# Attention before two mixture-of-experts layers: which engine computes the bias rows of the first tile, and how four PSUM banks are handed out

## Chip, cores, metric

The program runs on 1 core of one Trainium2 chip. The metric is the device time of one execution in microseconds (us); lower is better.

## What is computed

The reference, cut to the attention, where the change is. Batch B = 2, heads H = 8, sequence S = 576, head size D = 64.

```python
scores = scale * np.matmul(q, k.transpose(0, 1, 3, 2))
psi_rel = np.log1p(np.abs(pos[:, None] - pos[None, :]))
psi_i = np.log1p(np.maximum(pos[:, None], 1.0))
x = (psi_rel / psi_i)[..., None]
h = np.maximum(x @ w1 + b1, 0.0)          # 32 hidden units
bias = h @ w2                             # one number per head
scores = scores + bias.transpose(2, 0, 1)[None]
attn = np.exp(scores - scores.max(-1, keepdims=True))
attn = attn / (attn.sum(-1, keepdims=True) + 1e-09)
attn_out = np.matmul(attn, v)
```

The result goes through a first feed-forward layer and a second one with 8 experts, of which each token uses two. The change touches neither.

## The kernel before

**Tiling of the attention.** The 576 queries are cut into tiles of 128 (t = 0 to 3) and a rest of 64 per batch element. `BLOCKS` is the list of (batch, tile), the tile outermost, so the two batch elements share a tile's bias. A step of the main loop is a "pair" p: one block and two heads. There are 36 pairs.

**The bias.** The bias of a tile comes from 8 groups G of 16 queries. For a group, `bias_relu` writes four rows of 128 x 576 (g = 0 to 3): each is a shifted window of a table `wl`, plus a constant per partition, under a relu. Then `bias_mm` (L1048) multiplies them by `w2b` into PSUM, `bias_copy` scales the result into an SBUF tile `bt`, and `bias_store` (L1069, queue of SP) carries it by DMA into the tile `bias`. Groups 0 to 7 make the bias of tile t = 0, without which no pair can begin its softmax. Groups 8 and 9 follow right behind, and group 10 + p is made during pair p, for tiles 1 to 3.

**Who makes the rows.** For G < `POOLED` = 5, ACT makes row 3 (L1036) and DVE rows 0 to 2 (L1038). They lie in the later probability buffers (`pp`, even groups) or in four buffers `u` (odd groups). For G >= 5 POOL makes all four rows (L1034) in eight buffers `up`, that is, it can be two groups ahead of TensorE (PE). POOL has no add with relu here: it computes min and max with the constant, so the group's constant is negated (L995) and what is missing is added in the copy (`self.c`, L1060 on ACT for tile 0, L1062 on DVE after it). The first tile is computed in the order of groups 0, 5, 1, 2, 6, 3, 4, 7.

**A pair.** `qk` (L1138) writes the scores of two heads into two PSUM tiles `sc` (there are two such tiles of two banks each). `add_bias` (L1149, DVE) adds the bias and finds the extremum, `exp` (L1162, ACT) writes `pp`, `inv` (L1169 to L1172, DVE) makes the reciprocal of the sum, `tp` (L1181, L1183, PE) transposes the probabilities in three tiles of 128 x 384 or 512, `tp_copy` (L1189, ACT) copies each out as `pts`, `pv` (L1206, PE) multiplies them by v, and `pv_out` (L1217, DVE) writes the result. On PE the order of a steady pair is: `qk` of the next pair, three `tp`, two halves of a group's `bias_mm`, `pv`.

**The four PSUM banks.** The transposes, the halves of the bias from group 8 on, and the `pv` output all take a tile named `m` from the pool `ps_m` with four buffers of one bank each. All have one name, so the pool picks one of the four that it holds to be free when a tile is asked for.

**What sets the order.** Each engine runs its instructions in the order in which they are issued. A planner (`Plan`) takes the list of steps with costs, dependencies and keys, and fixes that order before the program runs. For the planner, tiles `m` go strictly in turn (`slot("m", 4)`); which bank a tile really gets is the pool's choice.

Of the kernel before, what the change touches and what calls it, by code (L numbers as in the profile page):

```python
# [9 lines left out]
F32 = mybir.dt.float32  # L10
# [8 lines left out]
P = 128  # L19
# [19 lines left out]

WL1 = TABS[0][0] - 103 - P  # L40

POOLED = 5


def group_of(G):
# [926 lines left out]
class Attn:  # L972
    def __init__(self, ctx, tc, t, xa, xb, ident):
        self.tc, self.nc = tc, tc.nc
        self.t = t
        self.ident = ident
        self.xa, self.xb = xa, xb
        nc = self.nc
        cp = ctx.enter_context(tc.tile_pool(name="aconst", bufs=1))
        self.wk = ctx.enter_context(tc.tile_pool(name="awork", bufs=2))  # L980
        self.early = ExitStack()
        self.wk2 = self.early.enter_context(tc.tile_pool(name="aearly", bufs=2, side="right"))
        self.ps_sc = ctx.enter_context(tc.tile_pool(name="ps_sc", bufs=2, space=bass.MemoryType.PSUM))
        self.ps_m = ctx.enter_context(tc.tile_pool(name="ps_m", bufs=4, space=bass.MemoryType.PSUM))
        self.small = small = cp.tile([P, SMALL], F32, name="small")
        nc.sync.dma_start(small, t["small"])

        self.wl = cp.tile([P, TABS[0][1]], F32, name="wl")
        nc.scalar.dma_start(self.wl[:, WL1:], t["psi0"][:, WL1:])
        self.w2b = small[:, 2:34]  # L990
        self.ninv = small[:, 34:34 + SEQ // 16]
        self.scb = small[:, 34 + SEQ // 16:-1]
        n = 4 * POOLED
        nc.vector.tensor_scalar(self.scb[:, :n], self.scb[:, :n], small[:, 1:2], None, op0=OP.mult)
        nc.vector.tensor_scalar(self.scb[:, n:], self.scb[:, n:], small[:, 1:2], -1.0, op0=OP.mult, op1=OP.mult)  # L995
        self.c = small[:, SMALL - 1:]
        self.scale_wl(slice(WL1, TABS[0][1]))

        self.kp = [cp.tile([P, 2, 4, SEQ], F32R, name=f"kp{b}") for b in range(2)]
        self.vt = [cp.tile([P, 4, 4, 2, 64], F32, name=f"vt{b}") for b in range(2)]  # L1000
        self.v5 = [cp.tile([P, 4, 2, 64], F32, name=f"v5{b}") for b in range(2)]

        self.bias, self.U, self.B, self.Q, self.S, self.PP, self.PT, self.X, self.raw = ({} for _ in range(9))

    def scale_wl(self, s):
        self.nc.vector.tensor_scalar(self.wl[:, s], self.wl[:, s], self.small[:, 0:1], None, op0=OP.mult)
# [2 lines left out]
    def groups(self, t):  # L1009
        return range(8 * t, min(8 * t + 8, SEQ // 16))  # L1010

    def constant(self):

        nc = self.nc
        cb = self.ps_m.tile([P, 512], F32, name="m")
        for g in range(4):
            nc.tensor.matmul(cb[32 * g:32 * g + 32, 0:1], self.w2b, self.small[:, 1:2], start=True, stop=True)
        nc.vector.tensor_scalar(self.c, cb[:, 0:1], -1.0, None, op0=OP.mult)
# [22 lines left out]
    def bias_mm(self, G, halves):  # L1041
        if len(halves) == 2:
            bp = self.ps_sc.tile([P, 2, 512], F32, name="sc")
        else:
            bp = self.ps_m.tile([P, 512], F32, name="m")[:, None, :]
        for k, n in enumerate(halves):
            for g in range(4):
                self.nc.tensor.matmul(bp[32 * g:32 * g + 32, k, :288], self.w2b,  # L1048
                                      self.U[G, g][:, n * 288:(n + 1) * 288], start=True, stop=True)
        self.B[G, halves] = bp  # L1050
# [123 lines left out]
    def tp(self, blk, c, k):  # L1174


        p = self.PP[blk, c][0]
        pt = self.ps_m.tile([P, 512], F32, name="m").rearrange("p (a b) -> p a b", a=4)
        for j in range(3):
            o = (3 * k + j) * P  # L1180
            self.nc.tensor.transpose(pt[:, j, :], p[:, o:o + P], self.ident)  # L1181
        if k == 2:
            self.nc.tensor.transpose(pt[:, 3, :], self.X.pop(("i", blk, c)).rearrange("p a b -> p (a b)"), self.ident)  # L1183
        self.PT[blk, c, k] = pt
# [7 lines left out]
    def pv(self, blk, c):  # L1192

        self.PP.pop((blk, c))
        pts = [self.PT.pop((blk, c, k)) for k in range(3)]
        xt = self.ps_m.tile([P, 512], F32, name="m")[:, :P]
        self.X[blk, c] = xt, pts[2][:, 3, :]
        for b, o, n in self.parts(blk):
            cs = slice(o, o + n)
# [28 lines left out]
    def run(self, late, moe):  # L1228
# [28 lines left out]
        def rows(G, key):  # L1257
            t, i, _ = group_of(G)
            us = []
            for g in range(4):  # L1260
                us.append(slot("up", 8) if G >= POOLED else slot("u", 4) if G % 2 else ("pp", g // 2, g % 2))
                e = "POOL" if G >= POOLED else "ACT" if g == 3 else "DVE"
                add(e, {"ACT": .67, "DVE": .43, "POOL": .75}[e], self.bias_relu, (G, g, e), [("wl", 0)] if t > 1 else [],
                    [us[-1]], key + .1 * g)
            return us

        def group(G, us, key):
# [12 lines left out]
        q(0)  # L1280
        kc(0, 0)

        for i, G in enumerate((0, 5, 1, 2, 6, 3, 4, 7)):
            group(G, rows(G, i - 9.7), i - 9)
            if i == 3:
                kc(0, 1, [("st", 2)])
# [22 lines left out]
        def v(b, c, after=()):  # L1309
            add("SP", 1.1, self.load_v, (b, c), list(after), [("v", b, c)], 4 * b + c - 1, 2.0)  # L1310

        qk(0)
        landed = [("st", 7)]
        v(0, 0, landed)
# [152 lines left out]
```

## Time and profile before

| | us |
|---|---|
| runs shown, median of 3 | 685.68 (684.35 to 686.38) |
| profiled execution, own time | 689.21 |
| its span in the trace | 687.5 |
| PE busy | 654.7 (95%) |
| DVE busy | 458.0 (67%) |
| ACT busy | 342.9 (50%) |
| POOL busy | 180.9 (26%) |

The profiled execution took 3.5 us longer than the median of the runs, and 1.7 us of its own time lie outside the span. The attention fills about the first 199 us; the two feed-forward layers follow. Shares of busy time are means over stages with quite different limits, so the rows below are those of single stretches.

### The profile page before, as it was taken

How to read it: one execution, taken by the hardware profiler on the slowest of the kernel's cores; microseconds unless marked ns; L12 is line 12 of the kernel's file. 1: busy time of each engine (PE TensorE's matmuls, PEld its weight loads, DVE VectorE, ACT ScalarE, POOL GpSimd, SP SyncE). 2: the span in 40 equal slices, each digit the busy share in tenths (PEclk: the TensorE clock that was granted, in tenths of full speed). 3: DMA queues.
4: the chain of work that ended last, by engine and by line, in shares of the span. 5: the costliest groups of instructions: out<-in, count | busy, mean ns of one | idle time of the engine just before them, and what ended most of it. 6: DMA issues, size and time to landing. Idle time of an engine off the chain costs nothing.

```text
span 687.5 us, 14783 instructions
## 1 busy us (share of the span) xinstructions
PE 654.7 (95%) x5777; PEld 553.0 (80%) x5777; DVE 458.0 (67%) x1010; ACT 342.9 (50%) x657; POOL 180.9 (26%) x215
## 2 busy tenths in 40 slices
PE   6799999999999998999999999999999999999992
PEld 2467766777789987999988997898888889888881
DVE  7589887976879878946656435565656465565621
ACT  5367766676674333445545345544434444444420
POOL 6867655541000000000042003103133140403311
PEclk9889999999999999999999999999999999999997
DMA  3785862326356787735245404658585776858521
GB/s 115 200 231 167 272 208 69 91 54 212 110 185 184 224 242 240 247 89 184 77 155 157 128 31 139 214 185 257 173 247 172 239 215 198 273 174 270 167 66 40
DMA packets 41629, 118.60 MB, mean 173 GB/s; under 512 B 6100, under 2 KB 6356, under 8 KB 39506
## 3 DMA queue, kind: packets, MB, share of 16 engines
q1 hardware_dynamic: 36850, 105.47, 49.8%
q0 software_dynamic: 4560, 11.71, 5.1%
q8 instruction: 47, 0.77, 0.5%
q10 hardware_dynamic: 144, 0.41, 0.2%
q14 instruction: 28, 0.23, 0.1%
HBM read 77.91 MB, written 30.75 MB: 158 GB/s over the span
## 4 chain that ended last, share of the span: by engine, by line
PE 79%; DVE 9%; DMA 5%; ACT 3%; issue 2%; POOL 0%; DVEq 0%; ACTq 0%; POOLq 0%
PE h L312 28%; PE acc L584 17%; PE m L1206 5%; PE sc L1138 5%; PE m L1181 4%; PE m L1048 4%; PE acc L344 4%; PE acc L342 3%; PE acc L343 3%; DMA wr<-in_w_in 3%; ACT pts L1189 2%; PE acc L523 1%; DMA wr<-in_w_out 1%; PE acc L380 1%; PE sc L1048 1%
## 5 line engine op out<-in xcount | busy, mean ns | idle before, releaser
L286 DVE TENSOR_TENSOR wlo<-wr,whi 128x1024 fp32r<-128x1024 f32 x96 | 117.1, 1222 | 55.9 <-ACT whi L283 51.4
L312 PE MATMUL h<-xah,whi 128*128 128x320 f32 x384 | 120.5, 314 | 0.3 <-DVE gg L329 0.3
L283 ACT ACTIVATE whi<-wr 128x1024 fp32r<-128x1024 f32 x96 | 101.2, 1056 | 36.4 <-PE acc L584 13.3
L312 PE MATMUL h<-xal,whi 128*128 128x320 f32 x384 | 119.1, 310 | 0.1
L312 PE MATMUL h<-xah,wlo 128*128 128x320 f32 x384 | 118.6, 309 | 0.0
L1034 POOL TENSOR_SCALAR up<-wl,small 128x576 f32<-128x576 f32 x124 | 96.9, 798 | 55.8 <-PE m L1048 46.0
L584 PE MATMUL acc<-whi,g 128*128 128x512 f32 x320 | 106.7, 398 | 0.0
L618 POOL DMA_INDIRECT out<-row x24 | 35.4, 1475 | 178.9 <-DVE row L609 140.2
L312 PEld LDWEIGHTS h<-xah,whi 128*128 128x128 f32 x384 | 72.4, 189 | 7.9 <-DVE gg L329 1.4
L558 ACT ACTIVATE g<-h 128x320 fp32r<-128x320 f32 x64 | 28.0, 437 | 98.8 <-PE h L312 43.9
L473 POOL DMA_INDIRECT xs<-rows,sidx x18 | 20.2, 1120 | 213.0 <-ACT lk L326 145.0
L312 PEld LDWEIGHTS h<-xal,whi 128*128 128x128 f32 x384 | 72.4, 189 | 4.5 <-DVE xal L545 0.9
L584 PE MATMUL acc<-wlo,g 128*128 128x512 f32 (+1 forms) x192 | 75.7, 395 | 0.0
L312 PEld LDWEIGHTS h<-xah,wlo 128*128 128x128 f32 x384 | 72.3, 188 | 0.0
L565 DVE SCALAR_TENSOR_TENSOR g<-h,g 128x64 fp32r<-128x64 f32 (+1 forms) x128 | 35.4, 318 | 51.9 <-ACT g L558 50.9
L1189 ACT ACTIVATE pts<-m 128x384 f32<-128x384 f32 (+1 forms) x108 | 50.0, 523 | 38.7 <-PE m L1181 35.2
L584 PEld LDWEIGHTS acc<-whi,g 128*128 128x128 f32 x320 | 56.9, 188 | 8.7
L344 PE MATMUL acc<-whi,g 128*128 128x512 f32 x144 | 56.8, 394 | 2.4 <-DVE g L333 2.4
L342 PE MATMUL acc<-whi,g 128*128 128x512 f32 x144 | 57.5, 399 | 0.0
L1162 ACT ACTIVATE pp<-s,mn 128x576 f32<-128x576 f32 x72 | 54.9, 767 | 5.1 <-DVE mn L1149 5.1
L343 PE MATMUL acc<-wlo,g 128*128 128x512 f32 x144 | 57.1, 396 | 0.0
L1149 DVE CUSTOM_DVE_ANT_0 s<-sc,bias 128x576 f32<-128x576 f32 x72 | 51.4, 747 | 1.1 <-PE sc L1138 1.1
(160 smaller groups left out, 1212.4 us busy)
## 6 DMA issues: line engine op xcount, KB each, us to landing
wr<-in_w SPq DMA_DIRECT2D x64, 512.0 KB
bias<-bt SPq DMA_DIRECT2D x40, 288.0 KB
wr<-in_w_in SPq DMA_DIRECT2D x8, 1024.0 KB
wr<-in_w_out SPq DMA_DIRECT2D x8, 1024.0 KB
wf<-wr SPq DMA_DIRECT2D x16, 512.0 KB
wr<-wf SPq DMA_DIRECT2D x16, 512.0 KB
row<-xs SPq DMA_DIRECT2D x23, 258.0 KB
xs<-xb SPq DMA_DIRECT2D x4, 1290.0 KB
```

Of the source, the lines that this page charges most:

```text
L283: self.nc.scalar.activation(w[0], r, AF.Copy)
L286: self.nc.vector.tensor_tensor(out=lo, in0=r, in1=hi.bitcast(F32), op=OP.subtract)
L312: self.nc.tensor.matmul(h, u[:, d, :], v[:, d, :], start=(d == 0 and i == 0), stop=(d == DC - 1 and i == 2))
L342: nc.tensor.matmul(acc, gh, whi, start=(f == 0), stop=False)
L343: nc.tensor.matmul(acc, gh, wlo, start=False, stop=False)
L344: nc.tensor.matmul(acc, gl, whi, start=False, stop=(f == self.FF1 // P - 1))
L565: self.nc.vector.scalar_tensor_tensor(gl, h[:, c], 0.0, g[:, c].bitcast(F32), op0=OP.max, op1=OP.subtract)
L584: nc.tensor.matmul(y, u, v, start=(f == 0 and i == 0), stop=(last and i == len(prods) - 1))
L1034: self.nc.gpsimd.tensor_scalar(u, w, 3.0e38, b, op0=OP.min, op1=OP.max)
L1149: self.nc.vector.tensor_tensor_reduce(out=s.rearrange("p (a b) -> p a b", a=2), in0=sc[:, :, :288], in1=bias[:, h, :].rearrange("p (a b) - ...
L1162: self.nc.scalar.activation(p[:, a * SEQ:(a + 1) * SEQ], s, AF.Exp, bias=mn[:, 0:1], scale=-1.0, accum_out=sm[:, 0, a:a + 1])
L1189: self.nc.scalar.activation(ps, self.PT[blk, c, k][:, :n, :], AF.Copy)
```

## The change

1. `POOLED` goes from 5 to 8. All groups of the first tile (0 to 7) now have three rows on DVE and one on ACT; POOL makes rows from group 8 on. The groups of the first tile run in the order 0 to 7.
2. The negation of POOL's constants, and the scaling of the 128 columns of `wl` that only later tiles read, move out of the set-up into a step `negate` on DVE. All POOL rows of tile 1 wait for it. It is planned behind row 2 of group 6; in the order that comes out it stands behind all 24 DVE rows.
3. The pool of four tiles `m` becomes four tiles m0 to m3 of one buffer each, and `bank()` takes them strictly in turn.

```diff
-POOLED = 5
+POOLED = 8
...
-        self.ps_m = ctx.enter_context(tc.tile_pool(name="ps_m", bufs=4, space=bass.MemoryType.PSUM))
+        self.ps_m = ctx.enter_context(tc.tile_pool(name="ps_m", bufs=1, space=bass.MemoryType.PSUM))
+        self.banks = 0
...
-        nc.vector.tensor_scalar(self.scb[:, n:], self.scb[:, n:], small[:, 1:2], -1.0, op0=OP.mult, op1=OP.mult)
         self.c = small[:, SMALL - 1:]
-        self.scale_wl(slice(WL1, TABS[0][1]))
+        self.scale_wl(slice(WL1 + P, TABS[0][1]))
...
+    def bank(self):
+
+        self.banks += 1
+        return self.ps_m.tile([P, 512], F32, name=f"m{self.banks % 4}")
...
+    def negate(self):
+
+        n = 4 * POOLED
+        self.nc.vector.tensor_scalar(self.scb[:, n:], self.scb[:, n:], self.small[:, 1:2], -1.0, op0=OP.mult, op1=OP.mult)
+        self.scale_wl(slice(WL1, WL1 + P))
...
-        cb = self.ps_m.tile([P, 512], F32, name="m")
+        cb = self.bank()
...
-            bp = self.ps_m.tile([P, 512], F32, name="m")[:, None, :]
+            bp = self.bank()[:, None, :]
...
-        pt = self.ps_m.tile([P, 512], F32, name="m").rearrange("p (a b) -> p a b", a=4)
+        pt = self.bank().rearrange("p (a b) -> p a b", a=4)
...
-        xt = self.ps_m.tile([P, 512], F32, name="m")[:, :P]
+        xt = self.bank()[:, :P]
...
-                add(e, {"ACT": .67, "DVE": .43, "POOL": .75}[e], self.bias_relu, (G, g, e), [("wl", 0)] if t > 1 else [],
-                    [us[-1]], key + .1 * g)
+                add(e, {"ACT": .67, "DVE": .43, "POOL": .75}[e], self.bias_relu, (G, g, e), [("neg", 0)] * (t > 0) + [("wl", 0)] * (t > 1),
+                    [us[-1], (f"row{G}.{g}", 0)], key + .1 * g)
...
-        for i, G in enumerate((0, 5, 1, 2, 6, 3, 4, 7)):
+        for i, G in enumerate(range(8)):
...
+        add("DVE", .5, self.negate, (), [("row6.2", 0)], [("neg", 0)], -2.2)
```

**What moves on DVE, at the start.** The order of the program before, from the first row of the bias to the first `add_bias` (`ql` and `kp` are the low halves of the split q and k):

```order
L1038 TENSOR_SCALAR pp<-wl,small 128x576 x3
L1038 TENSOR_SCALAR u<-wl,small 128x576 x3
L1109 SCALAR_TENSOR_TENSOR ql<-raw,qh 128x512
L1038 TENSOR_SCALAR pp<-wl,small 128x576 x3
L1083 TENSOR_TENSOR kp_97<-raw,kp_97 128x576
L1038 TENSOR_SCALAR u<-wl,small 128x576 x3
L1038 TENSOR_SCALAR pp<-wl,small 128x576 x3
L1062 TENSOR_SCALAR bt<-m,small 128x288 x2
L1083 TENSOR_TENSOR kp_97<-raw,kp_97 128x576
L1062 TENSOR_SCALAR bt<-m,small 128x288 x2
L1149 ISA s,mn<-sc,bias 128x576
```

The same stretch of the changed program (lines have shifted by 11; L1020 is the negation, the L1011 behind it the 128 columns of `wl`):

```order
L1049 TENSOR_SCALAR pp<-wl,small 128x576 x3
L1049 TENSOR_SCALAR u<-wl,small 128x576 x3
L1120 SCALAR_TENSOR_TENSOR ql<-raw,qh 128x512
L1094 TENSOR_TENSOR kp_96<-raw,kp_96 128x576
L1049 TENSOR_SCALAR pp<-wl,small 128x576 x3
L1020 TENSOR_SCALAR small<-small 128x112
L1011 TENSOR_SCALAR wl<-wl,small 128x128
L1094 TENSOR_TENSOR kp_96<-raw,kp_96 128x576
L1073 TENSOR_SCALAR bt<-m_303,small 128x288
L1073 TENSOR_SCALAR bt<-m_308,small 128x288
L1160 ISA s,mn<-sc,bias 128x576
```

Rows that repeat stand once: there are now eight triples of rows where there were five. The negation stands behind all of them, and one `bt` pair (group 9) now comes behind the two `add_bias`.

**What moves on PE, in two pairs of the middle.** Before, behind the last `qk` of a block in the second batch element, the three transposes of a pair and the bias halves behind them, with the semaphores that each waits for:

```order
L1181 MATMUL m<-ident,pp 128x128 [waits PE_49,Activation_49]
L1181 MATMUL m<-ident,pp 128x128 x2
L1181 MATMUL m<-ident,pp 128x128 [waits Activation_49]
L1183 MATMUL m<-ident,inv 128x128 [waits DVE_49]
L1048 MATMUL m<-up,small 32x288 [waits Pool_49] x4
L1048 MATMUL m<-up,small 32x288 x4
```

And the same pair now:

```order
L1192 MATMUL m_1768<-ident,pp 128x128 [waits PE_49,Activation_49]
L1192 MATMUL m_1780<-ident,pp 128x128 [waits DVE_49]
L1192 MATMUL m_1780<-ident,pp 128x128 [waits Activation_49]
L1192 MATMUL m_1786<-ident,pp 128x128 [waits DVE_49]
L1194 MATMUL m_1786<-ident,inv 128x128 [waits DVE_49]
L1059 MATMUL m_1796<-up,small 32x288 [waits DVE_49,Pool_49]
L1059 MATMUL m_1804<-up,small 32x288 [waits Activation_49]
```

Before, the second and the third transpose began with a wait for ACT alone; now they begin with a wait for DVE, as they do in the other pairs of both programs, and the wait for ACT inside the second is the one for the second head's `pp`. The pair after this one reads the same before and after.

## Rows read from the trace of the kernel before

**Rows 1.** The page, chain that ended last: shares of the span by engine.

```profile
PE 79%; DVE 9%; DMA 5%; ACT 3%; issue 2%; POOL 0%; DVEq 0%; ACTq 0%; POOLq 0%
```

**Rows 2.** DVE, the bias rows of L1038: duration ns min/median/max, first and last start us.

```profile
L1038 DVE TENSOR_SCALAR pp<-wl,small x9: 520/995/1002, 6.1 to 19.5; 128x576 f32<-128x576 f32 x9
L1038 DVE TENSOR_SCALAR u<-wl,small x6: 916/996/996, 8.3 to 16.8; 128x576 f32<-128x576 f32 x6
```

**Rows 3.** Timeline of DVE, first 21 us: start, us, what, count.

```profile
5.40 0.63 DVE L1006 TENSOR_SCALAR wl<-wl,small 128x807 f32<-128x807 f32 x1
...
11.09 0.68 DVE L1109 SCALAR_TENSOR_TENSOR ql<-raw,qh 128x512 fp32r<-128x512 f32 x1
...
14.36 0.74 DVE L1083 TENSOR_TENSOR kp<-raw,kp 128x576 fp32r<-128x576 f32 x1
...
17.70 2.83 DVE L1038 TENSOR_SCALAR pp<-wl,small 128x576 f32<-128x576 f32 x3
```

**Rows 4.** Timeline of POOL, its bias rows.

```profile
6.14 15.72 POOL L1034 TENSOR_SCALAR up<-wl,small 128x576 f32<-128x576 f32 x16 [4.76 <-DVE wl L1006]
22.44 2.90 POOL L1034 TENSOR_SCALAR up<-wl,small 128x576 f32<-128x576 f32 x4 [0.58 <-PE sc L1048]
...
40.57 3.92 POOL L1034 TENSOR_SCALAR up<-wl,small 128x576 f32<-128x576 f32 x4 [1.33 <-PE m L1048]
```

**Rows 5.** Timeline of ACT: a row, a copy, and the last copy of tile 0.

```profile
16.34 0.77 ACT L1036 ACTIVATE pp<-wl,small 128x576 f32<-128x576 f32 x1
17.01 0.82 ACT L1060 ACTIVATE bt<-sc,small 128x576 f32<-128x576 f32 x1
...
22.84 0.83 ACT L1060 ACTIVATE bt<-sc,small 128x576 f32<-128x576 f32 x1 [0.26 <-PE sc L1048]
```

**Rows 6.** Chain of waits in order of time, from the last store of tile 0.

```profile
23.70 3.65 DMA bias<-bt
...
27.38 0.98 DVE bt L1062 x2
28.36 0.66 DVE s L1149
```

**Rows 7.** Timeline of PE: groups 8 and 9, and the `qk` that open pairs.

```profile
24.71 2.15 PE L1048 MATMUL m<-up,small 128*32 128x288 f32 x32
29.18 1.50 PE L1138 MATMUL sc<-kp,qh 64*128 64x288 f32 x4 [2.32 <-DVE mn L1149]
...
37.01 0.54 PE L1138 MATMUL sc<-kp,qh 64*128 64x288 f32 x4
...
49.55 0.53 PE L1138 MATMUL sc<-kp,qh 64*128 64x288 f32 x4
```

**Rows 8.** Timeline of DVE: end of the `inv` that PE awaits before 49.55.

```profile
45.13 0.23 DVE L1172 COPY inv<-sm 128x128 f32<-128x128 f32 x1
```

**Rows 9.** Busy time by stretch: us, PE, PEld, DVE, ACT, POOL, granted clock, DMA, GB/s.

```profile
29.00:36.50 7.50, 7.22 (x66) 5.22 (x70) 4.21 (x14) 5.11 (x12) 3.65 (x6) 0.55 0.84 262
...
43.00:49.50 6.50, 4.94 (x63) 3.31 (x62) 5.55 (x14) 4.45 (x11) 3.33 (x3) 0.74 0.90 237
```

**Rows 10.** Timeline of PE: four `qk` in a row, and transposes between them.

```profile
94.47 0.54 PE L1138 MATMUL sc<-kp,qh 64*128 64x288 f32 x4
...
98.90 0.53 PE L1138 MATMUL sc<-kp,qh 64*128 64x288 f32 x4
...
101.09 0.55 PE L1181 MATMUL m<-ident,pp 128*128 128x128 f32 x3 [0.64 <-ACT pts L1189]
...
105.06 0.54 PE L1138 MATMUL sc<-kp,qh 64*128 64x288 f32 x4
...
111.21 0.54 PE L1138 MATMUL sc<-kp,qh 64*128 64x288 f32 x4
```

**Rows 11.** Timeline of ACT in the first of those two pairs.

```profile
99.88 0.63 ACT L1106 ACTIVATE qh<-raw 128x512 fp32r<-128x512 f32 x1 [0.90 <-PE sc L1138]
100.54 0.49 ACT L1189 ACTIVATE pts<-m 128x384 f32<-128x384 f32 x1
```

## Prediction

> **What bounds the kernel now.** I read the chain of waits first. PE carries 79% of it [rows 1], and in the middle of the attention PE runs without a gap in a fixed rhythm, but for two pairs (term 3): one `qk` to the next takes 98.90 - 94.47 = 4.43 us [rows 10]. So whatever delays PE early moves everything behind it, and the change can act in two places only: the head of the program, where PE waits for the bias of the first tile, and single pairs where PE waits for a bank. The feed-forward layers hang on the end of the attention (their first weight loads wait for buffers that it frees), so I carry a shift to the end in full.
>
> The head, in order. DVE makes 15 rows. The shortest took 520 ns, the middle one 995 [rows 2]; the short one is the very first, at 6.1, and POOL began its own rows at 6.14 [rows 4]. Three rows at 17.70 took 2.83, a pitch of (2.83 - 0.995)/2 = 0.92 [rows 3]. POOL's 16 rows took 15.72, 0.98 each, while four rows with DVE idle took 2.90, 0.725 each [rows 4]. The two engines slow each other; nothing else in the rows differs. DVE's last row ends at 17.70 + 2.83 = 20.53, ACT's last copy of tile 0 at 22.84 + 0.83 = 23.67 [rows 5], the store lands at 27.35, and DVE first spends 0.98 on a copy of group 9, so `add_bias` starts about 28.3 [rows 6]. PE, done with groups 8 and 9 at 26.86, stands still for 2.32 and starts the next `qk` at 29.18 [rows 7], with a granted clock of 0.55 until 36.5 [rows 9], mostly the lower of its two levels (1.2 GHz, not 2.4). That `qk` to the next takes 37.01 - 29.18 = 7.83 in place of 4.43.
>
> **Term 1, DVE's rows.** Nine rows are added (24 for 15), but POOL is silent beside them. The price of a row alone shows once: 0.52 long. Successive DVE rows overlap by 0.995 - 0.92 = 0.08, which makes the pitch 0.44; the scaling of `wl`, 807 columns in 0.63 just before POOL starts [rows 3], gives 0.45 for 576 columns. I take 0.44, with 0.52 as the upper end. Rows and the two splits between them (0.68 and 0.74 long [rows 3], 1.27 together less the overlap) are 24 x 0.44 + 1.27 = 11.8; begun at 5.97 (the scaling covers 679 columns, 0.1 shorter), DVE ends at 17.8, 2.7 earlier than now. At 0.52 it is 19.7. ACT does eight rows and eight copies at 0.67 a piece (17.01 - 16.34 [rows 5]), 10.7, plus three splits of some 0.6, from 5.9: 18.4 without any wait, and it waits some 1.5 for its first copies. So ACT is nearly as tight as DVE: the last copy ends at about 20.1 against 23.67, the store lands 3.65 later at 23.8, and `add_bias` begins there, since group 9's copy now stands behind it: 4.5 earlier.
>
> The Trainium skill ("SBUF — State Buffer", Who interferes with whom) says that of a DVE instruction that uses the pair of ports shared with GpSimd and a GpSimd instruction the later one blocks until the other is done. By that a DVE row beside a POOL row would cost up to 0.725 + 0.44 = 1.17, and taking POOL away would free 15 x 0.73 = 10.9 of DVE's time; the rows, at a pitch of 0.92, allow 15 x 0.48 = 7.2, and I use the rows.
>
> **Term 2, POOL's late start.** POOL's rows for group 8 begin not at 6.14 + 12 x 0.98 = 17.9, with the rows of three groups already behind them, but behind the negation, at 17.8 + 0.5 = 18.3, and now with DVE's rows out of the way. Eight rows at 0.725 to 0.80 (DVE's split of k falls among them) end at 24.1 to 24.7. Behind them PE's half of group 9 costs 2.15/2 = 1.1 [rows 7], or twice that at the lower clock: it ends at 25.2 to 26.8. PE runs in order, so the next `qk` stands behind it: 25.2 to 26.8 against 29.18 now, a second obstacle that gives back up to a microsecond of term 1. From group 10 on POOL needs 2.9 to 3.9 a group [rows 4] against PE's 4.43 a pair: hidden. The negation and the small scaling (about 0.5) move from before the first row to behind the last; at the start they save 0.2, counted above. SP issues the store of group 9 behind two loads of k and one of v instead of before them: nothing awaits that store before pair 8, so nothing.
>
> Head together: PE's second `qk` 2.4 to 4.4 earlier. I take **-4.0**, because the lower figure needs the slow clock already at group 9, and because DVE, no longer held by group 9's copy, does `add_bias` 4.5 earlier.
>
> **Term 3, the banks.** From 98.90 three successive `qk` stand 6.16 and 6.15 apart (105.06, 111.21) where 4.43 is the rule [rows 10]. Inside each, the second and third transposes wait 0.64 for ACT's copy of the one before: three tiles in one bank, copied out one after the other, while three banks are free. With the turn fixed, as in the order shown, neither begins with a wait for that copy. Gain: 6.16 + 6.15 - 2 x 4.43 = **-3.45**. In the first pair ACT also splits a q (99.88 to 100.51) before its first copy at 100.54 [rows 11]; three copies of 0.5 to 0.6 end by 102.2, when PE has also finished its halves of the bias, so no new wait shows. Everywhere else a bank comes back after four tiles already, and nothing changes. Lower end: 1.7, if one of the pairs keeps a wait.
>
> **Sum.** 689.21 - 4.0 - 3.45 = 681.76 for the profiled execution. The median of the runs is 3.53 lower; the shift is the same, so 685.68 - 7.45 = **678.2**.
>
> **Rivals.**
> - *The head gains more, because the clock comes up.* From `add_bias` at 28.3 to the `inv` that ends at 45.36 [rows 8] are 17.1 us, of which DVE is idle for 7.50 - 4.21 = 3.3 in the stretch with the clock at 0.55; a second dip to 0.74 follows at 43 to 49.5 [rows 9]. If PE stays at 2.4 GHz, DVE's own work is the floor: 23.8 + 13.8 + 1.0 (group 9's copy) = 38.6, 6.8 earlier. Then 685.68 - 6.8 - 3.45 = 675.4. For it: PE's gaps between 21 and 25 are 0.4 and about 1.9 (before groups 8 and 9) instead of 2.32 in one. Against: it is only about half busy there. Chance 0.17.
> - *POOL's late start eats the head.* DVE rows at 0.52, negation done at 20.2, POOL at 0.80 a row: group 9 ready at 26.6, PE done at the lower clock at 28.8, gain at most 0.4. Then only the banks count: 685.68 - 0.4 - 3.45 = 681.8. Chance 0.15.
> - *Slower: PE starved into the low clock.* PE waits for POOL's rows before groups 8, 9 and 10, and is busy half the time or less from 19 us on. If the low clock then holds for two pairs more than now, at 7.83 - 4.43 = 3.4 each, +6.8 stands against -3.45 from the banks and nothing from the head: 689.0. It decides if the gap before group 10 is still there, that is, if POOL's rows exceed 4.43/4 = 1.1 each; the worst seen is 3.92/4 = 0.98. The Trainium skill ("TensorE: Matmul & The Clock Gate", HAM oscillation) describes this: waits between bursts of matmuls make each next burst start at half clock. The dips at 29 and 43 agree with it. Chance 0.05.
> - *The banks do not do it.* The two long pairs have another cause (the q split, or DVE), and the waits return under another name: 685.68 - 4.0 = 681.7. Against: the wait is there in the second pair as well, which has no split. Chance 0.08.
>
> **How the numbers follow.** The forecast keeps 0.55. 678.2 is its time; its own range is 676.5 to 680 (the head at 2.4 to 4.5, the banks at 2.9 to 3.45). The range 674.5 to 682.0 takes in the other gains (675.4, 681.8, 681.7) and leaves out the slower case and the tails, under 0.2. What can be told from no change is about 0.3%, 2.06 us: faster means below 683.6. All cases but the slower one lie there, with some spill in the two near 681.8: faster 0.89, same 0.06, slower 0.05.
>
> **What would show it.** Right: DVE rows of the first tile at a pitch near 0.44 with POOL idle beside them; the last copy of tile 0 on ACT at about 20; first `add_bias` near 24 and the second `qk` near 25 to 26; no 0.64 waits of a transpose for ACT near 95, `qk` there 4.43 apart; the end of the attention 7 to 8 earlier and the rest unchanged in length. Wrong: rows still near 0.9 (then POOL was not the cause), a second `qk` at 28 or later behind POOL's rows, two pairs in the middle still 6 long, or a longer stretch at half clock before 60.

## The result, and the profile after

The changed kernel takes 677.69 us (median of 4 runs, 675.84 to 679.92), the one before, run beside it, 686.03 (4 runs): a ratio of 0.9884, interval 0.9849 to 0.9919. Two repeats of the same pair, with more runs, gave 0.9914 (0.9882 to 0.9947) and 0.9908 (0.9876 to 0.9940). In microseconds the three gains are 8.34, 4.85 and 6.30 by the medians, 6.5 on average, and 8.0, 5.9 and 6.3 by the ratios; forecast were 7.45. The forecast holds in sign and range, and each interval has room for 7.45. Of its two terms one is met in the traces to 0.01 us, and the other is larger than the repeats show; the rest of this text is about which, and why one pair of traces would have hidden it.

**Busy time.** The page of the changed kernel, own time 675.84, span 674.1 (before: 689.21 and 687.5):

```profile
PE 647.4 (96%) x5777; PEld 549.8 (82%) x5777; DVE 453.9 (67%) x1020; ACT 343.2 (51%) x660; POOL 169.2 (25%) x203
```

POOL gave up 12 rows, and DVE, which does nine of them, is not busier than before (458.0): it makes 24 rows in less time than 15 took. The timeline of DVE (start, us, what, count, and in brackets the idle time before and what ended it) shows how:

```profile
5.41 1.38 DVE L1049 TENSOR_SCALAR pp<-wl,small 128x576 f32<-128x576 f32 x3
...
15.83 1.38 DVE L1049 TENSOR_SCALAR pp<-wl,small 128x576 f32<-128x576 f32 x3 [1.12 <-PE sc L1059]
17.12 1.37 DVE L1049 TENSOR_SCALAR u<-wl,small 128x576 f32<-128x576 f32 x3
18.41 0.28 DVE L1020 TENSOR_SCALAR small<-small 128x112 f32<-128x112 f32 x1
...
25.31 0.76 DVE L1160 CUSTOM_DVE_ANT_0 s<-sc,bias 128x576 f32<-128x576 f32 x1 [0.95 <-DMA bias<-bt]
```

Three rows take 1.38 instead of 2.83 [rows 3]: a pitch of (1.38 - 0.52)/2 = 0.43. The last row ends at 18.5 (before 20.53), although DVE has stood 1.12 for PE, and POOL begins only behind the negation, as its timeline shows:

```profile
18.99 15.99 POOL L1045 TENSOR_SCALAR up<-wl,small 128x576 f32<-128x576 f32 x20 [17.61 <-DMA raw<-in_kd]
```

The first `add_bias` starts at 25.31 instead of 28.28 (the chain of [rows 6] has 28.36). ACT waits for PE ahead of four of its copies (L1069) and for a load ahead of a split of k (L1092), 3.36 in all. That split stands ahead of the last copy of tile 0, which starts at 20.70 and ends at 21.42 (before 22.84 and 23.67 [rows 5]). A later split waits for its load as well:

```profile
9.03 0.74 ACT L1069 ACTIVATE bt<-sc,small 128x576 f32<-128x576 f32 x1 [1.18 <-PE sc L1059]
...
10.97 0.74 ACT L1069 ACTIVATE bt<-sc,small 128x576 f32<-128x576 f32 x1 [0.54 <-PE sc L1059]
...
13.63 0.74 ACT L1069 ACTIVATE bt<-sc,small 128x576 f32<-128x576 f32 x1 [0.62 <-PE sc L1059]
...
16.28 0.74 ACT L1069 ACTIVATE bt<-sc,small 128x576 f32<-128x576 f32 x1 [0.58 <-PE sc L1059]
...
20.11 0.68 ACT L1092 ACTIVATE kp<-raw 128x576 fp32r<-128x576 f32 x1 [0.44 <-DMA raw<-in_kd]
20.70 0.72 ACT L1069 ACTIVATE bt<-sc,small 128x576 f32<-128x576 f32 x1
...
32.81 0.69 ACT L1092 ACTIVATE kp<-raw 128x576 fp32r<-128x576 f32 x1 [1.64 <-DMA raw<-in_kd]
```

PE, in its timeline, runs from group 8 into the second `qk` without a wait, at 26.41 against 29.18, and reaches the third one 5.20 later, not 7.83 [rows 7]. The wait that is new comes in the pair behind it:

```profile
22.46 4.02 PE L1059 MATMUL m<-up,small 128*32 128x288 f32 x32
26.41 0.99 PE L1149 MATMUL sc<-kp,qh 64*128 64x288 f32 x4
...
31.61 0.53 PE L1149 MATMUL sc<-kp,qh 64*128 64x288 f32 x4
...
34.31 0.77 PE L1192 MATMUL m<-ident,pp 128*128 128x128 f32 x5 [1.05 <-ACT pp L1173]
...
37.99 0.53 PE L1149 MATMUL sc<-kp,qh 64*128 64x288 f32 x4
...
43.02 0.54 PE L1149 MATMUL sc<-kp,qh 64*128 64x288 f32 x4
```

The wait for ACT at 34.31 is the wait for a load, one step on: ACT makes that `pp` behind the split at 32.81. The chain of waits has it as

```profile
26.59 6.20 DMA raw<-in_kd
32.81 0.69 ACT kp L1092
```

The clock, by windows (us, then PE, PEld, DVE, ACT, POOL, granted clock, DMA share, GB/s), does not fall where it stood at 0.55 before [rows 9]; it reads 1.00 in every such window from 16 to 52:

```profile
28.00:32.00 4.00, 4.00 (x72) 2.76 (x73) 3.88 (x10) 2.73 (x6) 4.00 (x6) 1.00 1.06 297
32.00:36.00 4.00, 2.50 (x26) 1.68 (x26) 2.40 (x6) 2.42 (x6) 2.98 (x4) 1.00 1.03 285
```

In the middle of the attention the two long pairs of [rows 10] are gone: 96.83 - 92.39 = 4.44, 101.26 - 96.83 = 4.43, and the three transposes run as one burst of nine matmuls with no wait for ACT:

```profile
92.39 0.53 PE L1149 MATMUL sc<-kp,qh 64*128 64x288 f32 x4
...
96.83 0.54 PE L1149 MATMUL sc<-kp,qh 64*128 64x288 f32 x4
...
97.82 1.20 PE L1192 MATMUL m<-ident,pp 128*128 128x128 f32 x9
...
101.26 0.54 PE L1149 MATMUL sc<-kp,qh 64*128 64x288 f32 x4
```

**Where the 13.4 us between the two traces lie.** The start of certain steps (us), for these two kernels and five of the traces told below:

| trace | 2nd `qk` | 3rd | 5th | 6th | feed-forward (L312) | its first layer done (L523) |
|---|---|---|---|---|---|---|
| before | 29.18 | 37.01 | 49.55 | 53.97 | 199.2 | 418.9 |
| before, again (e9) | 28.50 | 35.21 | 45.71 | 50.14 | 195.4 | 415.1 |
| banks alone (e1) | 28.64 | 35.35 | 47.89 | 52.31 | 194.1 | 412.9 |
| rows alone (e2) | 26.53 | 35.64 | 45.11 | 49.54 | 195.8 | 414.0 |
| changed | 26.41 | 31.61 | 43.02 | 47.46 | 189.2 | 405.4 |
| changed, again (e5) | 25.74 | 31.55 | 42.72 | 47.15 | 189.9 | 406.6 |
| changed, third (e10) | 25.81 | 31.50 | 42.76 | 47.19 | 189.7 | 404.8 |

From before to changed: 6.5 up to the sixth `qk`, 10.0 by the start of the feed-forward (the banks' 3.44 more), 13.5 at L523. From L523 to the end all take 268.5 to 268.8. So 3.5 us come from the stage between 199 and 419, where both run the same instructions. Over the traces of this study that stage takes between 404.8 - 189.7 = 215.1 and 221.5. The three traces of the changed kernel lie lowest (215.1 to 216.7) and both of the kernel before at 219.7, but three variants of the changed kernel told below (e7, e11, e12) take 219.2 to 220.7, and the medians of the runs leave no room for 13.4. So they are not counted as a gain of the change; what sets the length of that stage was not tested.

The second trace of the kernel before is the better base. Against it the changed kernel's repeats start the sixth `qk` 3.0 us sooner and the feed-forward 5.5 to 5.7 sooner, close to what the medians give. And 0.7 of the first trace's lateness is there before anything of the change can act: its first row of the bias starts at 6.06, and those of the other traces between 5.28 and 5.83. In e9, by the timeline of DVE:

```profile
5.36 2.36 DVE L1038 TENSOR_SCALAR pp<-wl,small 128x576 f32<-128x576 f32 x3
```

### The profile page after: what moved, and what is told of

It is laid out like the page before. It is cut to its first block, busy times and chain, and to the rows that moved or that the text cites. A ratio compares the mean times of both kernels' runs of the same rounds, so it can differ in the third digit from the quotient of the medians.

```text
span 674.1 us, 14782 instructions
## 1 busy us (share of the span) xinstructions
PE 647.4 (96%) x5777; PEld 549.8 (82%) x5777; DVE 453.9 (67%) x1020; ACT 343.2 (51%) x660; POOL 169.2 (25%) x203
## 4 chain that ended last, share of the span: by engine, by line
PE 79%; DVE 7%; DMA 6%; ACT 3%; issue 2%; SPq 0%; POOL 0%; ACTq 0%; DVEq 0%; POOLq 0%
PE h L312 28%; PE acc L584 18%; PE m L1217 5%; PE sc L1149 5%; PE m L1192 4%; PE acc L344 4%; PE acc L342 4%; PE acc L343 3%; PE m L1059 3%; DMA wr<-in_w_in 2%; ACT pts L1200 2%; DMA raw<-in_kd 2%; PE acc L523 1%; DMA wr<-in_w_out 1%; PE sc L1059 1%
## 5 line engine op out<-in xcount | busy, mean ns | idle before, releaser
L312 PE MATMUL h<-xah,whi 128*128 128x320 f32 x384 | 119.9, 312 | 0.0
L312 PE MATMUL h<-xal,whi 128*128 128x320 f32 x384 | 118.8, 309 | 0.1
L312 PE MATMUL h<-xah,wlo 128*128 128x320 f32 x384 | 118.4, 308 | 0.0
L1045 POOL TENSOR_SCALAR up<-wl,small 128x576 f32<-128x576 f32 x112 | 85.1, 777 | 57.7 <-PE m L1059 35.6
L312 PEld LDWEIGHTS h<-xah,whi 128*128 128x128 f32 x384 | 72.1, 188 | 6.6 <-ACT xah L543 0.3
L312 PEld LDWEIGHTS h<-xal,whi 128*128 128x128 f32 x384 | 72.1, 188 | 4.6 <-DVE xal L545 0.9
L312 PEld LDWEIGHTS h<-xah,wlo 128*128 128x128 f32 x384 | 72.1, 188 | 0.0
```

The costliest lines, as they stand in the source:

```text
L312: self.nc.tensor.matmul(h, u[:, d, :], v[:, d, :], start=(d == 0 and i == 0), stop=(d == DC - 1 and i == 2))
L1045: self.nc.gpsimd.tensor_scalar(u, w, 3.0e38, b, op0=OP.min, op1=OP.max)
```

## The experiments

Two measurements of parts, one of the cause, then clock, the new wait, and repeats. Ratios are to the kernel before on the same chip, 686.08, 685.44 and 685.55 us in the three groups of runs (e1 to e4, e5 to e8, e9 to e12).

**e1, the banks alone.** The program before with part 3 of the change:

```diff
-cb = self.ps_m.tile([P, 512], F32, name="m")
+cb = self.bank()
```

> The kernel before with the third part of the change alone: four named banks strictly in turn; POOL still makes the rows of groups 5 to 7. Bank theory: the two long pairs near 99 and 105 us (6.16 and 6.15 from one qk to the next) shrink to the usual 4.43, nothing else moves: the end of the attention 3.45 us earlier, the ratio to the kernel before about 0.995. Rival (the long pairs come from the split of a q on ACT, or from DVE): at least one of the two keeps a wait, and the gain is 1.7 us or nothing.

682.01 us, ratio 0.9929 (0.9903 to 0.9955): 4.1 less, interval 3.1 to 6.7. In its timeline of PE

```profile
97.24 0.53 PE L1144 MATMUL sc<-kp,qh 64*128 64x288 f32 x4
...
101.68 0.54 PE L1144 MATMUL sc<-kp,qh 64*128 64x288 f32 x4
...
106.11 0.54 PE L1144 MATMUL sc<-kp,qh 64*128 64x288 f32 x4
```

the two pairs take 4.44 and 4.43: 6.16 + 6.15 - 8.87 = 3.44. The bank theory stands. Its sixth `qk` is 1.66 ahead of the first trace of before, with the same head: a first sign of how much the head varies (0.55 of it is the later first row of that trace, 6.06 against 5.51).

**e2, the rows alone.** The changed program with the old pool:

```diff
-self.ps_m = ctx.enter_context(tc.tile_pool(name="ps_m", bufs=1, space=bass.MemoryType.PSUM))
+self.ps_m = ctx.enter_context(tc.tile_pool(name="ps_m", bufs=4, space=bass.MemoryType.PSUM))
...
-        return self.ps_m.tile([P, 512], F32, name=f"m{self.banks % 4}")
+        return self.ps_m.tile([P, 512], F32, name="m")
```

> The change without the named banks: first and second part alone, one pool of four buffers as before. If the two halves of the change add up without touching each other: the head as in the changed kernel (DVE rows near 0.44 apart, qk of pair 4 about 6.5 us earlier than before), the two long pairs still 6.1 to 6.2 us, together 6 to 7 us faster than the kernel before in the profile (ratio about 0.990 to 0.991). Rival (the head's gain is mostly a luckier clock in one profile): pair 1 to 2 again near 7.8 us in this run, and a gain of 3 to 4 us (ratio about 0.995).

683.84 us, ratio 0.9969 (0.9941 to 0.9998): 2.2 less, interval 0.1 to 4.0, below both expectations. The two pairs are back at 6.15 and 6.15, with the old wait of 0.64 under the new line. PE's timeline shows both, and a new wait in the head:

```profile
31.69 0.47 PE L1194 MATMUL m<-ident,inv 128*128 128x128 f32 x1 [2.49 <-DVE inv L1183]
...
97.69 0.55 PE L1192 MATMUL m<-ident,pp 128*128 128x128 f32 x3 [0.64 <-ACT pts L1200]
```

PE waits 2.49 for an `inv` that in the changed kernel's trace came in time. The timeline of DVE shows why, and that of POOL beside it:

```profile
27.92 3.25 DVE L1180 TENSOR_SCALAR sm<-sm 128x2 f32<-128x2 f32 x1
```

```profile
18.97 12.18 POOL L1045 TENSOR_SCALAR up<-wl,small 128x576 f32<-128x576 f32 x16 [17.58 <-DMA raw<-in_kd]
```

A DVE step on two columns takes 3.25 us, and ends at 31.17, just when POOL's run of rows ends, at 18.97 + 12.18 = 31.15. The same step takes 0.42 in the changed kernel at 27.77, and 0.73 at most in all 36 of e5's trace. Behind the wait the clock falls (0.64 in the window 32 to 36) and the pair takes 9.11. So the same head can lose 4 us in one pair by one such step; at the fifth `qk`, 45.11 against 43.02, 2.1 of them are left.

**e3, POOL beside DVE again, for groups 8 and 9 only.** Rows on DVE and banks as changed; the negation goes back to the start, so that POOL begins at once:

```diff
+nc.vector.tensor_scalar(self.scb[:, n:], self.scb[:, n:], small[:, 1:2], -1.0, op0=OP.mult, op1=OP.mult)
...
-self.scale_wl(slice(WL1 + P, TABS[0][1]))
+self.scale_wl(slice(WL1, TABS[0][1]))
...
-add("DVE", .5, self.negate, (), [("row6.2", 0)], [("neg", 0)], -2.2)
```

> The changed kernel with the negation and the whole scaling of the table back in the set-up, so that POOL makes its rows of groups 8 and 9 at once, beside DVE's rows of the first tile. Contention theory: for the 8 POOL rows (about 8 us) DVE's rows stand 0.9 apart instead of 0.44, DVE's last row comes 3 to 4 us later than in the changed kernel, and the qk of pair 1 lies 1.5 to 3 us later, although POOL is ready with group 9 some 10 us sooner. Rival (the order and the sharing out of the rows matter, not POOL beside DVE): DVE's rows stay below 0.6, and the qk of pair 1 comes up to 1 us earlier than in the changed kernel, as it no longer stands behind POOL's rows of group 9.

681.93 us, ratio 0.9935 (0.9907 to 0.9963): by the ratios 1.9 us behind e10 ((0.9935 - 0.9908) x 686), with intervals that overlap, and level with e1, the banks alone (0.9929). The trace says more. One kernel now shows both prices, here DVE's rows, then POOL's eight:

```profile
8.12 2.84 DVE L1050 TENSOR_SCALAR u<-wl,small 128x576 f32<-128x576 f32 x3
...
14.15 1.36 DVE L1050 TENSOR_SCALAR u<-wl,small 128x576 f32<-128x576 f32 x3
```

```profile
5.91 8.01 POOL L1046 TENSOR_SCALAR up<-wl,small 128x576 f32<-128x576 f32 x8 [4.52 <-DVE wl L1012]
```

While POOL works, to 13.92, three rows take 2.84; right behind it, 1.36. The second `qk` is at 29.20, 2.8 later than in the changed kernel, and no sooner than in the kernel before (29.18 and 28.50). PE's timeline has it:

```profile
29.20 0.36 PE L1150 MATMUL sc<-kp,qh 64*128 64x288 f32 x1 [1.57 <-DVE mn L1161]
```

That POOL is what made DVE's rows long is shown. And with POOL at work beside DVE the other parts of the change, the order of the groups and the sharing out of the rows, bring nothing to the head.

**e4 and e6, PE kept busy in its wait.** On top of e1, 14 or 4 matmuls behind group 9 whose result nobody reads:

```diff
+        for _ in range(14):
+            self.nc.tensor.matmul(w[:32, :288], self.w2b, self.wl[:, 500:788], start=True, stop=True)
```

> The kernel before with named banks, and 14 matmuls of 128 x 288 whose result nobody reads behind group 9, where TensorE stands still for 2.3 us before the qk of pair 1: about 1.9 us of work that fills the gap. Clock theory (the pairs 1 and 2 were slow because the clock fell in that gap): granted clock near 1.0 instead of 0.55 from 29 to 36 us, pair 1 to 2 in 4.5 to 5.5 us instead of 7.8, and 2 to 3.5 us gained against the run with the named banks alone. Rival (the clock is down for another reason, or DVE is the limit there anyway): pair 1 to 2 still over 6.5 us, or a gain at pair 2 that is lost again at pair 4, so that the end of the attention lies within 0.7 us of the run with named banks alone.

> As the run with 14 idle matmuls on top of the kernel before with named banks, but with 4 of them: at the 0.25 us that each of its 28 passes took there, they last 2.0 us and fit into the 2.3 us gap. Clock theory: qk of pair 1 near 28.5 to 29.0 as without them, granted clock 1.0 up to 36, pair 1 to 2 in 4.4 to 5.2 us, qk of pair 4 at 44.5 to 46.5 against 47.9 without them, so 1.5 to 3 us faster than the run with the named banks alone. Rival (DVE is the limit up to pair 4 whatever the clock): qk of pair 4 at 47.3 or later, no gain over the named banks alone.

e4: 684.29 us, ratio 0.9968 (0.9948 to 0.9987), by the medians 2.3 behind e1, where 2 to 3.5 were to be gained. The 14 matmuls, 28 instructions in the trace, took 6.95 us, 0.25 an instruction, where the bias halves' 0.07 [rows 7] would have made 1.9; they held the second `qk` back to 32.92, 4.3 behind e1. Yet the next is 4.43 later, with the clock at 1.00 throughout, and the fifth `qk` (48.32) is 0.4 behind e1. Part of what was lost came back with the clock; how much of it came from loads and DVE steps that could run ahead meanwhile, e4 does not tell. The timeline of PE, the added matmuls and the `qk` behind them:

```profile
26.04 6.95 PE L1015 MATMUL m<-wl,small 128*32 128x288 f32 x28
32.92 0.53 PE L1150 MATMUL sc<-kp,qh 64*128 64x288 f32 x4
```

e6: 680.61 us, ratio 0.9918 (0.9888 to 0.9949). Four matmuls fill 2.1 of the 2.3 us in which e1's PE stood still. Its second `qk` comes at 28.51, as in e1, and the fifth at 45.27, 2.6 sooner. PE's timeline:

```profile
28.51 0.37 PE L1150 MATMUL sc<-kp,qh 64*128 64x288 f32 x1 [0.41 <-DVE mn L1161]
...
34.75 0.53 PE L1150 MATMUL sc<-kp,qh 64*128 64x288 f32 x4
...
45.27 0.54 PE L1150 MATMUL sc<-kp,qh 64*128 64x288 f32 x4
```

The windows from 28 to 36, e1 first, then e6:

```profile
28.00:32.00 4.00, 3.04 (x22) 2.62 (x22) 2.92 (x10) 2.61 (x6) 3.77 (x6) 0.84 0.87 244
32.00:36.00 4.00, 4.00 (x68) 2.45 (x68) 2.71 (x7) 3.29 (x7) 1.51 (x2) 0.73 0.87 297
```

```profile
28.00:32.00 4.00, 3.38 (x35) 2.52 (x38) 2.92 (x10) 2.96 (x8) 3.64 (x6) 1.00 0.85 239
32.00:36.00 4.00, 3.19 (x65) 2.08 (x55) 3.54 (x9) 2.85 (x7) 3.35 (x4) 1.00 0.95 328
```

So it is the gap of 2.3 us on PE that lets the clock fall. What that costs is less sure. The pair is 6.24 long at full clock, against 6.71 in e1 and in e9 (below): of the 2.3 us that theirs has over 4.43, 0.5 went with the clock, and the rest is waiting (0.76 for a load of v, in e6). At the fifth `qk` e6 is 2.6 ahead of e1 but only 0.4 ahead of e9, which has the gap too (45.71). In time e6 can't be told from e1, nor from the changed kernel (0.9914 and 0.9908).

**e5, the changed kernel again.** No edit.

> The changed kernel once more, unaltered, so that its time rests on more than four runs and its head is seen in a second profile. Theory (head 4 to 4.5 us on the median, more only when the clock stays up in the profile, plus 3.45 from the banks): median 7.5 to 8.5 us below the kernel before, ratio 0.9875 to 0.989; the two middle pairs again 4.43; the qk of pair 4 between 43.0 us (clock up, as in the first profile) and 45.5 (clock down once, as in the run without named banks). Rival (the two parts do not add up, as the run with the rows alone gained only 2.2): median 5.5 to 6.5 below.

680.59 us (9 runs), ratio 0.9914 (0.9882 to 0.9947), 4.85 less than before: less than either expectation by the medians, while the ratio's 5.9 is inside the second. The trace repeats the first one within 0.7 us up to the feed-forward.

**e7, the k loads sooner.** They wait for earlier stores:

```diff
-kc(0, c, landed)
+kc(0, c, [("st", c + 1)])
```

> The changed kernel with the third and the fourth load of k allowed behind the stores of groups 3 and 4 instead of group 7, so that SP issues both before the store of group 9. If the changed kernel's new bound is the fourth load of k (issued at 26.6, landed at 32.8, ACT waits 1.64 us for it in the profile and TensorE 1.05 us behind that): no wait of the split of k on ACT, pair 2 to 3 in 4.4 to 5.4 us instead of 6.4, qk of pair 4 at 41.5 to 42.5, 0.5 to 1.5 us gained. Rival (DVE's own work is the bound there, the wait for the load is covered): qk of pair 4 within 0.4 us of 43.0, nothing gained.

681.14 us, ratio 0.9923 (0.9888 to 0.9957): missed. The order changed with the load: DVE's half of that split now stands ahead of an `add_bias`, and PE, in its timeline, waits for that instead:

```profile
33.18 0.52 PE L1149 MATMUL sc<-kp,qh 64*128 64x288 f32 x3 [1.72 <-DVE mn L1160]
```

The clock fell behind it (0.72 in 32 to 36), and the fifth `qk` came at 44.39, 1.4 late.

**e8, one DVE step less per pair.** The sum's addition of 1e-9 before the reciprocal is left out.

```diff
-v.tensor_scalar(sm[:, 1, :], sm[:, 0, :], 1e-9, None, op0=OP.add)
...
-v.reciprocal(sm[:, 1, :], sm[:, 1, :])
+v.reciprocal(sm[:, 1, :], sm[:, 0, :])
```

> The changed kernel without the addition of 1e-9 to the sums (the only part left out; the sums are at least 1 and in fp32 stay as they are). That step on two columns took 0.15 us at best, 0.5 to 0.7 beside POOL's rows, and once 3.25 us behind four POOL rows in the run with the rows alone. If DVE's chain to the reciprocals bounds the pairs of the head: qk of pair 4 0.5 to 1.5 us earlier than in the changed kernel with the clock in the same state, and no DVE step of two columns over 1 us; later pairs unchanged at 4.43, since TensorE bounds them. Rival (DVE does not bound the head): no difference beyond the spread of the two profiles of the changed kernel.

679.79 us (6 runs), ratio 0.9893 (0.9844 to 0.9941), no difference from the changed kernel that can be told; fifth `qk` at 43.14, no sooner. PE's waits there are much as they were: 0.76 for ACT at 34.15, behind the load of k, and 1.04 for DVE's `inv` at 40.68.

**e9 and e10, both programs again, on one chip.** No edit.

> The program before, unaltered, traced a second time: how much of the difference between the two first traces is the draw and not the change? Theory A (the head of before is much the same each time): second qk at 28.6 to 29.3, fifth at 47.9 to 49.6, the two middle pairs 6.15 each, feed-forward starting 195 to 200. Theory B (the first trace of before was an unlucky draw): fifth qk at 46 or less, feed-forward starting near 193. The stage from there to the first layer's end takes 216 to 222 by either, with no tie to the program.

> The changed program, unaltered, on the same chip and with the same runs of before as the others of this call. Theory A (head about 4 and banks 3.45): 7.5 below before, 5.5 to 9.5. Theory B (the head is worth 1 to 2 in the median of many runs, as the repeat's 4.85 had it): 4 to 6 below. In the trace the fifth qk at 42.7 to 45.1 and the middle pairs at 4.43 by both.

e9: 684.46 us (12 runs), a ratio of 0.9983 (0.9965 to 1.0000) to its own program: 1 us is what such a comparison can miss by. In its trace, the timeline of PE, the head lies between the two theories:

```profile
28.50 0.37 PE L1138 MATMUL sc<-kp,qh 64*128 64x288 f32 x1 [2.33 <-DVE mn L1149]
...
35.21 0.53 PE L1138 MATMUL sc<-kp,qh 64*128 64x288 f32 x4
...
45.71 0.53 PE L1138 MATMUL sc<-kp,qh 64*128 64x288 f32 x4
```

The wait of 2.33 is the same, but the pair behind it takes 6.71, not 7.83 (clock 0.78 and 0.79 in the windows from 28 to 36, where the first trace had 0.62 and 0.53), and the second dip, 0.75 at 44 to 48 in the first trace, is not there. So 3.8 us of the 6.5 by which the first two traces differ at the sixth `qk` is the draw of the first trace of before (0.7 of it the later first row).

e10: 679.25 us (10 runs), ratio 0.9908 (0.9876 to 0.9940): 6.3 less, inside theory A's range and just over theory B's. Against e9's trace the sixth `qk` is 50.14 - 47.19 = 2.95 sooner.

**e11 and e12, what holds the second `qk`?** First the split of k behind the last copy, then also group 9 behind the second `qk` on PE:

```diff
-add("ACT", .58, self.split_k, (b, c, 0), [r], [("k0", b, c)], k)
+add("ACT", .58, self.split_k, (b, c, 0), [r] + [("cp", 7)] * ((b, c) == (0, 1)), [("k0", b, c)], k)
...
+            if p == 0:
+                group(9, u9, 1.05)
```

> The changed program with ACT's split of the second k tile behind its last copy of tile 0 instead of ahead of it. Theory A (the second qk hangs on the bias of the first tile): last copy about 0.7 to 1.0 earlier (19.7 to 20.0 in place of 20.70), add_bias near 24.4, second qk 0.7 to 1.0 earlier, about 25.5. Theory B (the second qk hangs on group 9, whose rows POOL ends late): add_bias near 24.4 as well, yet the second qk stays at 26.1 to 26.4. Time within 1 us of the changed program by both.

> As the run before, and with PE's halves of group 9 behind the second qk instead of ahead of it. Theory A (bias bound): no earlier than the run before. Theory B (POOL's late rows are what holds the second qk): second qk at 24.9 to 25.4, right behind the first add_bias, 1.0 to 1.5 earlier than in the changed program; group 9 then costs its 1.0 to 1.2 of PE in the next pair, where PE waits for the softmax anyway. The third k load still sets the fourth qk, so the time gains at most 1 us, under what can be told; if the clock falls in the gap, it loses 2 to 3.

e11: 679.52 us, ratio 0.9899 (0.9867 to 0.9931). Its last copy is 0.93 earlier than in the first trace of the changed kernel, yet `add_bias` only 0.17, as ACT's and DVE's timelines show:

```profile
19.77 0.74 ACT L1069 ACTIVATE bt<-sc,small 128x576 f32<-128x576 f32 x1 [0.55 <-PE sc L1059]
```

```profile
25.14 0.76 DVE L1160 CUSTOM_DVE_ANT_0 s<-sc,bias 128x576 f32<-128x576 f32 x1 [1.68 <-DMA bias<-bt]
```

From the copy's end to `add_bias` it is now 25.14 - 20.51 = 4.63, where the changed kernel had 25.31 - 21.42 = 3.89. In e5 and e10, the same kernel unaltered, `add_bias` starts at 24.72 and 24.80, 3.89 and 3.79 behind the copy, and so sooner than in e11. Both theories had `add_bias` at 24.4, and both missed: the store took back what the copy gained. What makes the store longer when it starts sooner stays open; from 21 to 23 us the DMA share is 0.97 in e11 and 0.64 to 0.73 in the three traces of the changed kernel, so that transfers in each other's way are a guess, which no run tests.

e12: 679.96 us, ratio 0.9920 (0.9894 to 0.9946). With group 9 out of the way PE stands still for 3.18, and the second `qk` comes no sooner than in e11 (26.05), as PE's timeline shows; beside it the window from 28 to 32:

```profile
26.20 0.37 PE L1149 MATMUL sc<-kp,qh 64*128 64x288 f32 x1 [3.18 <-DVE mn L1160]
...
33.95 0.54 PE L1149 MATMUL sc<-kp,qh 64*128 64x288 f32 x4
...
43.50 0.54 PE L1149 MATMUL sc<-kp,qh 64*128 64x288 f32 x4
```

```profile
28.00:32.00 4.00, 4.00 (x31) 2.25 (x34) 3.48 (x10) 1.65 (x4) 1.71 (x3) 0.62 0.95 300
```

So POOL's late rows don't hold it, and its own theory B falls. But the clock now drops to 0.62, and the next `qk` takes 7.75 in place of e11's 31.77 - 26.05 = 5.72 (group 9's own matmuls, moved there, are a part of that). In the changed kernel it is group 9, trickling in as POOL makes its rows, that keeps PE at full clock through its wait for the bias. What that is worth is small by the fifth `qk`: 43.50, against 42.90 in e11 and 42.72 to 43.02 in the changed kernel, and the times can't be told apart.

None of these is clearly ahead of the changed kernel: the intervals of e5, e6, e8, e10, e11 and e12 overlap. Matmuls that fill the gap on top of the changed kernel were not tried, since its PE has no gap there.

## Why the prediction was right, and where it was off

- **Term 1, DVE's rows: right.** Pitch 0.43 against the 0.44 taken. DVE's last row ends at 18.5 against 17.8: it began 0.56 sooner than assumed and waited 1.12 for PE (0.63 and 0.70 in e5 and e10), a wait that the sum did not have. The cause, contention with POOL, is shown by e3 (2.84 beside POOL, 1.36 behind it, and no gain at the second `qk`). By the Trainium skill's rule ("SBUF — State Buffer", Who interferes with whom) a DVE row would have cost up to 1.17, the prediction's estimate (0.725 + 0.44). That is not what the row shows there: e3's pitch is 0.92 again. For a small step it can be worse than one POOL instruction: in e2 one DVE step seems to have waited through some four POOL rows of about 0.76 (12.18/16).
- **The step from there to `add_bias`: this is the step that failed.** Forecast were 23.8 and 4.5 us sooner. It starts at 25.31, and at 24.72 and 24.80 in e5 and e10; against e9, where it starts at 27.61, that is 2.3 to 2.9 sooner. The term that was too small is "it waits some 1.5 for its first copies": ACT waits 3.36 before its last copy, 2.92 for PE and 0.44 for the load behind a split of k that the prediction counted among "three splits" and not as a wait. The last copy ends at 21.42 where 20.1 was forecast (20.83 and 21.01 in e5 and e10). The store's 3.65 was nearly right, 3.8 to 3.9 up to `add_bias`. But e11, which takes that split away, shows that it is no constant: there the copy ends at 20.51, and the store takes 4.63.
- **The head's -4.0: too large.** It was chosen because `add_bias` was to come 4.5 sooner. Term 2's own bounds, 25.2 to 26.8 against 29.18, make 2.4 to 4.0, not "2.4 to 4.4", so it was their best case. Measured at the second `qk` are 2.8 in the first pair of traces and 2.1 to 2.8 against e9; at the sixth, against e9, 2.7 to 3.0. By the ratios the rows are worth 2.1 alone (e2) and 1.0 to 3.1 where the banks alone (e1) are taken off the three comparisons; the intervals are too wide to rule out 4.0 (e2's ends there). Behind the head a new wait takes part of the gain back: the load of k, issued at 26.59 and landed at 32.8 with the DMA share at 1.03 to 1.06, makes the third pair 6.38 long. The prediction carried its shift through the pairs behind the second `qk` as if they stayed as they were.
- **Term 2, POOL's late start: priced right, read wrong.** PE's second `qk` at 26.41 lies in the forecast 25.2 to 26.8. It was called a second obstacle that gives back up to a microsecond of term 1. It gives back 0.2 at most: from `add_bias` to the second `qk` it is 1.0 to 1.1 in the three traces of the changed kernel and 0.91 in e12, without group 9's matmuls ahead of it. What they do there is to keep the clock up.
- **Rival 1, the clock comes up: right as to the clock, not as to its size.** It was held back by "it is only about half busy there". The clock stayed at 1.00 in the traces of the changed kernel, e5 and e10, with 4.0 us of matmuls between 22.46 and 26.41. The Trainium skill ("TensorE: Matmul & The Clock Gate", HAM oscillation) has it that waits between bursts make the next burst begin at half clock; e12's 3.18 us of waiting and 0.62 behind it agree, and e6's filled gap at 1.00. Its size, 6.8, was met by the first two traces at the fifth `qk` (6.5) and is not the typical one (e10 against e9: 2.95). It came from the first trace of before, where "the next `qk` takes 7.83 in place of 4.43" and a dip at 43 to 49.5 follows; e9 shows 6.71 and no second dip.
- **Term 3, the banks: right.** 3.44 in e1's trace and in the changed one, -3.45 forecast; 4.1 by medians, interval 3.1 to 6.7. e2 has the long pairs without it. The rival that the two pairs have another cause falls.
- **Rival "POOL's late start eats the head" (681.8) and the slower one (689.0):** POOL's rows took 0.80 each (15.99/20), under the 1.1 at which the slower case was to decide, and DVE's rows 0.43, not 0.52. e2 shows that one unlucky DVE step can take back as much of the head as the first of them had, by another path: its second `qk` is on time, at 26.53.
- **The sum and its range.** "676.5 to 680" does not follow from the bounds beside it: a head of 2.4 to 4.5 and banks of 2.9 to 3.45 make 677.7 to 680.4. That the first comparison gave 8.34, more than the forecast although the head was priced too high, is luck: its interval is 5.6 to 10.4, and the repeats gave less. The traces flatter the change further: those of the changed kernel are each of the shortest run of their set (675.84, 677.05 and 675.14 us), and the first trace of before was 3.5 above its median. That "the rest" stays "unchanged in length" is not what the first two traces show (3.5 us in the feed-forward stage), and against e9 the feed-forward starts 5.5 to 6.2 us sooner, where the end of the attention was to come 7 to 8 sooner.

## What to carry to other kernels

Before a stall in one trace is priced, trace the unaltered kernel a second time: here 3.8 of 6.5 us were the draw, and an experiment set against one trace (e6 against e1) can mislead in the same way. When two engines do the same elementwise work at the same time, compare the time of a row alone and beside the other; giving all of it to the faster engine can be quicker than sharing (24 rows in 13.1 us against 15 in 14.5, splits included). When an engine's end is summed from its steps, look for what each step waits for: ACT's waits were 3.4 us, not 1.5. And before a gap on PE is called idle time, look at the clock behind it: work that trickles through a wait can hold the clock, and moved out of the wait it need not save anything (e12).

## What the runs showed of the hardware that was not expected

- A DVE step on 128x2 lasted 3.25 us while POOL ran rows back to back (e2), against 0.15 at best and 0.73 at most in the 36 such steps of e5's trace. That POOL held it is read from the two ends, 31.17 and 31.15, and was not tested by itself.
- Matmuls that write the same 32 partitions of one PSUM tile one after the other took 0.25 us each (e4: 6.95/28), while the bias halves, which go round four groups of 32 partitions, took 2.15 for 32, 0.07 each [rows 7].
- Two us of matmuls without use (e6) keep the clock at 1.00 where e1 and e9 show 0.73 to 0.84. The fifth `qk` comes at 45.27, against 47.89 in e1 and 45.71 in e9. By the ratios e6 is 0.8 us below e1 ((0.9929 - 0.9918) x 686), which the intervals can't tell from nothing.
